# Batch 0: three V chunks normalised on ScalarE, and the magnitudes of six pieces of w_out taken there

## The chip, the cores and the metric

One core of a Trainium2 chip runs the whole program. Its engines are TensorE (PE for matmuls, PEld for weight loads), VectorE (DVE), ScalarE (ACT), GpSimd (POOL) and SyncE (SP, which here issues nearly all DMAs). Each has a queue of its own and runs it strictly in the order in which it was built; the engines meet at semaphores. The metric is the device time of one execution in microseconds.

## What is computed

Three layers run one after the other on 4 batches of 576 rows: windowed causal attention with ALiBi bias (8 heads of 64), a gated MLP with a spatial mix (the part that this change touches), and a second MLP with a three-tap convolution as its gate.

```python
h = gelu(x @ w_in)                       # 512 -> 1024
u, v = h[..., :512], h[..., 512:]
v_n = (v - mean(v)) / np.sqrt(var(v) + 1e-6) * g_ln
v_s = np.einsum('ts,bsd->btd', w_sg, v_n) + b_sg[None, :, None]
x = x + (u * v_s) @ w_out
```

The weights of the matmuls come as float64. The kernel reads their bits as pairs of 32-bit words and makes two fp32r parts of each, high and low, so that a product is three matmuls (high by high, high by low, low by high).

## The kernel before

The rows of `V` of a batch (its 576 positions) are cut into five chunks, `V0.0` to `V0.4` for batch 0: four of 128 rows and a last one of 64 rows. `m_v` makes a chunk: matmuls into a PSUM bank, the gelu on ACT into the tile `v`, mean and variance on DVE (L767, L768), one over the root on POOL (L770, L771, a power of -0.5), `(v - mean) * rs` on DVE in one instruction (L772), and the split: the high part `vn` is a cast on ACT (L223), the low part a subtraction on DVE (L232). The last chunk is first put together from two halves of a bank, by a copy on ACT (L223) and an addition on DVE.

`m_u` makes `u` in halves of 256 and 320 rows with a gelu on ACT from a bank; `m_sg` is the spatial mix (`pss`, evicted by DVE at L829); `m_wo` the product with `w_out` (`pso`). These, and `m_v`, share a pool of two PSUM banks: a group of matmuls can't begin until the bank it gets has been read by an engine. The scores of the attention (`sc`) take banks from another pool, are masked by DVE (L440, with the row maximum) and put through exp on ACT with a row sum; L487 and L488 invert the sums, and POOL and DVE scale the weights by them (L243, tiles `t`).

While batch 0 is in its gated MLP, the weights `w_sg` (five pieces, `g0` to `g4`) and `w_out` (eight pieces of 256 columns, `o0.0` to `o3.1`) are brought in and split between the other steps, and the scores and exps of batch 1 are made. A piece of `w_out` goes through `narrowed`: its high words without sign (L313 on DVE, or L311 on ACT where `act_abs` is set), a clamp (L317), a mask and shift (L318), two steps that put in the sign and the low bits (L319, L320), all on DVE; then a cast on ACT (high part, `wo`) and a subtraction on POOL (low part). The tile `wa` has two buffers, so the first instruction of a piece waits until the piece two before it is through ACT and POOL.

`_steps` lists the order of steps, for batch 0's MLP `g0 g1 V0.2 g2 o0.0 U0.0.3 g3 o0.1 V0.4 ... o1.0 C o1.1 V0.3 o2.0 o2.1 U0.1.0 ...`; from it, the framework's scheduler sets the order of each engine's instructions by a time line of its own, so an edit to one instruction can move its neighbours. `pick` and `book` keep an account of each engine's work, by which some copies and splits choose an engine. The functions follow with the line numbers of the profile.

Of the kernel before, what the change touches and what calls it, by code (L numbers as in the profile page):

```python
# [11 lines left out]
AF = mybir.ActivationFunctionType  # L12
ALU = mybir.AluOpType
# [122 lines left out]
def attention_gmlp_glu_kernel(  # L136
# [21 lines left out]
    nc = tc.nc  # L158
    PSUM = bass.MemoryType.PSUM

    def f(ap):
        return ap.bitcast(F32)

    def pad(pool, n, name):

        if n:
            pool.tile([P, 8 * n], F32, name=name, bufs=1)
# [16 lines left out]
    def act(*args, **kw):  # L184

        book("act", (225 if "accum_out" in kw else 60) + width(args[0]))
        ins = nc.scalar.activation(*args, **kw)  # L187
        if last_act:
            tc.add_manual_dep(ins.ins, last_act[-1], follow, reason="tables")
        last_act.append(ins.ins.name)  # L190
        return ins
# [4 lines left out]
    def width(ap):  # L196
        n = 1
        for d in ap.shape[1:]:
            n *= d
        return n  # L200

    def book(eng, ns):
        load[eng] = max(load[eng], load["pe"] - SLACK) + ns

    def pick(costs):
        eng = min(costs, key=lambda e: max(load[e], load["pe"] - SLACK) + costs[e])
        book(eng, costs[eng])
        return eng

    def mm(out, lhsT, rhs, start, stop, **kw):  # L210
        per = 2 if lhsT.dtype == F32 else 1
        book_pe = max(width(rhs), 2 * width(lhsT) if per == 1 else width(lhsT)) * per / 2.4
        load["pe"] += book_pe
        return nc.tensor.matmul(out, lhsT, rhs, start=start, stop=stop, **kw)  # L214

    def copy(dst, src, psum=False, engines="act dve pool"):
        n = width(src)
        cost = dict(act=52 + 0.85 * n, dve=67 + 1.04 * n) if psum else dict(
            act=20 + 1.0 * n, dve=150 + 0.52 * n, pool=130 + 0.9 * n
        )  # L220
        eng = pick({e: c for e, c in cost.items() if e in engines.split()})
        if eng == "act":
            return nc.scalar.copy(dst, src)  # L223
        if eng == "dve":
            return nc.vector.tensor_copy(dst, src)
        return nc.gpsimd.tensor_scalar(dst, src, 1.0, 1.0, op0=ALU.mult, op1=ALU.mult)  # L226

    def tt(dst, a, b, op, engines="dve pool"):
        n = width(a)
        cost = dict(dve=67 + 1.045 * n, pool=147 + 2.1 * n)  # L230
        eng = pick({e: c for e, c in cost.items() if e in engines.split()})
        return (nc.vector if eng == "dve" else nc.gpsimd).tensor_tensor(dst, a, b, op=op)  # L232
# [12 lines left out]
    def split(hi, lo, src, kind=None, done=None):  # L245

        ins = copy(hi, src, kind is None, ON[kind + " hi"] if kind else "act dve")
        if done is not None:
            done[:] = [ins.ins.name]
        return tt(lo, src, f(hi), ALU.subtract, ON[kind + " lo"] if kind else "dve")  # L250
# [11 lines left out]
    with tc.using_default_side("right"):  # L262
        pa = ExitStack()
        apool = pa.enter_context(tc.tile_pool(name="apool", bufs=2))
# [13 lines left out]
    for i in range(NP):  # L278
        st = cpool.tile([P, 18], F32, name=f"st{i}")
# [19 lines left out]
    def narrowed(src, n, pool, tag, bufs, spool, stag, sbufs, act_abs=False):  # L299

        if spool is None:
            st = src
        else:
            st = spool.tile([P, STAGE[stag]], U32, tag=stag, name="w64", bufs=sbufs)
            dma = nc.sync.dma_start(st[:, : 2 * n], src)
            later(dma)
        words = st[:, : 2 * n].rearrange("p (n w) -> p n w", w=2)
        low, high = words[:, :, 0], words[:, :, 1]
        a = pool.tile([P, 256 if tag == "wa" else 512], U32, tag=tag, name="wa", bufs=bufs)[:, :n]
        if act_abs:  # L310
            tc.keep_in_program_order(nc.scalar.activation(f(a), f(high), AF.Abs))  # L311
        else:
            ins = tc.keep_in_program_order(nc.vector.tensor_scalar(a, high, 0x7FFFFFFF, None, op0=ALU.bitwise_and))  # L313
            if last_hi:
                tc.add_manual_dep(ins.ins, last_hi[-1], follow, reason="high part first")
        clamp = nc.gpsimd if pick({e: c for e, c in dict(dve=67 + 0.52 * n, pool=147 + 0.93 * n).items() if e in ON["clamp"]}) == "pool" else nc.vector
        tc.keep_in_program_order(clamp.tensor_scalar(f(a), f(a), W_LOW, W_HIGH, op0=ALU.max, op1=ALU.min))  # L317
        nc.vector.tensor_scalar(a, a, 0x07FFFFFF, 3, op0=ALU.bitwise_and, op1=ALU.logical_shift_left)  # L318
        nc.vector.scalar_tensor_tensor(a, high, 0xC0000000, a, op0=ALU.bitwise_and, op1=ALU.bitwise_or)  # L319
        nc.vector.scalar_tensor_tensor(a, low, 29, a, op0=ALU.logical_shift_right, op1=ALU.bitwise_or)  # L320
        book("dve", 200 + 2.6 * n)
        return f(a)

    def cols(w, k, c0, n):

        return w.bitcast(U32)[:, k, 2 * c0 : 2 * (c0 + n)]
# [3 lines left out]
    def later(dma):  # L330

        tc.add_manual_dep(dma.ins, last_in[0].ins.name, follow, reason="later")
# [14 lines left out]
    def staged(src, dtype):  # L347
        st = mpool.tile([P, S], dtype, tag="x", name="wst", bufs=8)[:, : src.shape[-1]]
        later(nc.sync.dma_start(st, src))
        return st  # L350
# [11 lines left out]
    def w_out_piece(k, half):  # L362
        if k == half == 0:
            kept["wo"] = w1pool.tile([P, NK, 2, 2, 256], F32R, tag="wo", name="wo")
        st = staged(cols(w_out, k, half * 256, 256), U32)
        a = narrowed(st, 256, apool, "wa", 2, None, "x", 8)
        split(kept["wo"][:, k, half, 0, :], kept["wo"][:, k, half, 1, :], a, "wo")

    p2pool = []
# [365 lines left out]
    def m_v(b, j):  # L735
        ps = gps.tile([P, 512], F32, tag="g", name="psv")

        r = P if j < 4 else 64
        half, o = j // 2 if j < 4 else 1, j % 2 * P
        if j < 4:  # L740
            work = [(a[:, o : o + P], w, P) for k in range(NK) for hi, lo in [xg[b, k, half]] for a, w in ((hi, winh), (hi, winl), (lo, winh))]
            work = [(a, w[:, i // 3, HF:], n) for i, (a, w, n) in enumerate(work)]
        else:
            xt = [mpool.tile([P, 320], F32R, tag="t1", name="xt", bufs=NT1)[:, :P] for _ in range(NK)]
            for k in range(NK):
                copy(xt[k].rearrange("p (a n) -> p a n", a=2), xtail[b, k], engines="pool")
            work = [(xt[k], winh[:, k, HF:], P) for k in range(NK)]
            work += [(xt[k][:, :D], winl[:, k, HF:], D) for k in range(NK)]
        for n, (a, w, rows) in enumerate(work):
            mm(ps[:rows], a, w, start=n == 0, stop=n == len(work) - 1, skip_group_check=j == 4)  # L750
        if j < 4:
            vn = mpool.tile([P, 2, HF], F32R, tag="vn", name="vn", bufs=NVN)
            hi, lo = vn[:, 0, :], vn[:, 1, :]
        else:
            if b == 0:
                pad(mpool, 6, "pad1")
            hi = lo = mpool.tile([P, HF], F32R, tag="vt", name="vn", bufs=1)
        v = mpool.tile([P, HF], F32, tag="v", name="v", bufs=NV)
        if j < 4:
            act(v, ps, AF.Gelu_apprx_tanh)  # L760
        else:
            copy(v[:r], ps[r:], True, "act")
            tt(v[:r], ps[:r], v[:r], ALU.add, "dve")
            act(v[:r], v[:r], AF.Gelu_apprx_tanh)
        bs, ba, rs = small(6, "bs"), small(2, "ba"), small(1, "rs")
        book("dve", 1200)
        nc.vector.bn_stats(bs[:r], v[:r])  # L767
        nc.vector.bn_aggr(ba[:r], bs[:r])  # L768
        book("pool", 800)
        nc.gpsimd.tensor_scalar(rs[:r], ba[:r, 1:2], 1.0, 1e-6, op0=ALU.mult, op1=ALU.add)  # L770
        nc.gpsimd.tensor_tensor(rs[:r], rs[:r], mhalf[:r], op=ALU.pow)  # L771
        nc.vector.tensor_scalar(v[:r], v[:r], ba[:r, 0:1], rs[:r], op0=ALU.subtract, op1=ALU.mult)  # L772
        split(hi[:r], lo if j < 4 else hi[64:], v[:r], "vn first")
        vns[b, j] = (hi, lo)

# [79 lines left out]
    def constants(i):  # L855
# [10 lines left out]
    STEP = dict(  # L866
        k=constants, l=z_load, v=z_vload, c=z_scores, e=z_exp, n=z_norm, t=z_transpose, z=z_av, j=w_in_load, L=a_load, M=a_vload, C=a_scores, E=a_exp, N=a_norm, T=a_transpose, A=a_av,
        X=a_xsplit, V=m_v, U=m_u, G=m_sg, W=m_wo, i=w_in_piece, g=w_sg_piece, o=w_out_piece, a=w2_piece,
    )

# [228 lines left out]
```

## Time and profile before

| | us |
|---|---|
| runs shown (3): lowest, median, highest | 550.97, 551.67, 553.74 |
| the execution that was profiled | 552.74 |
| its span, first to last instruction | 550.7 |

The profiled execution took 552.74 us, 2.04 us more than its span, and 1.07 us more than the median of the three. On the page, busy time is given by engine and share of the span. A timeline gives instructions in order of time, equal neighbours merged, with the idle time of the engine before them and what ended it. A matmul's duration is modelled, and starts of neighbours on one engine may lie closer together than a duration, as writing back overlaps with the next instruction.

### The profile page before, as it was taken

How to read it: one execution, taken by the hardware profiler on the slowest of the kernel's cores; microseconds unless marked ns; L12 is line 12 of the kernel's file. 1: busy time of each engine (PE TensorE's matmuls, PEld its weight loads, DVE VectorE, ACT ScalarE, POOL GpSimd, SP SyncE). 2: the span in 40 equal slices, each digit the busy share in tenths (PEclk: the TensorE clock that was granted, in tenths of full speed). 3: DMA queues.
4: the chain of work that ended last, by engine and by line, in shares of the span. 5: the costliest groups of instructions: out<-in, count | busy, mean ns of one | idle time of the engine just before them, and what ended most of it. 6: DMA issues, size and time to landing. Idle time of an engine off the chain costs nothing.

```text
span 550.7 us, 12017 instructions
## 1 busy us (share of the span) xinstructions
PE 524.9 (95%) x4560; PEld 476.3 (86%) x4560; DVE 371.9 (68%) x955; ACT 263.2 (48%) x681; POOL 249.4 (45%) x379
## 2 busy tenths in 40 slices
PE   8997979999999999999999989998999999999997
PEld 7776778898898988998897979997997999999887
DVE  4999898655869766879766688597577434664300
ACT  6694577342457542376444524473544333444311
POOL 2444239451237262345534344177496454455500
PEclk9999999899999999999999999998999999999999
DMA  8973440333250864322553423901201300100111
GB/s 296 384 245 155 148 153 24 137 119 109 80 182 24 247 201 150 122 80 75 188 186 97 139 87 124 336 8 43 82 18 43 103 21 19 42 20 19 39 38 58
DMA packets 33209, 63.93 MB, mean 116 GB/s; under 512 B 3968, under 2 KB 13952, under 8 KB 33152
## 3 DMA queue, kind: packets, MB, share of 16 engines
q1 hardware_dynamic: 33008, 63.04, 34.4%
q8 instruction: 36, 0.59, 0.4%
q14 instruction: 21, 0.17, 0.1%
q10 hardware_dynamic: 144, 0.13, 0.1%
HBM read 48.47 MB, written 14.68 MB: 115 GB/s over the span
## 4 chain that ended last, share of the span: by engine, by line
PE 47%; DVE 21%; ACT 11%; POOL 10%; DMA 5%; issue 4%; SPq 0%; POOLq 0%; ACTq 0%; DVEq 0%
PE psg L214 26%; PE pso L214 6%; ACT t L187 5%; PE psu L214 4%; DMA x2d<-x 3%; PE psv L214 3%; POOL t L243 3%; PE o L214 3%; POOL gl L232 2%; DVE cc L957 2%; PE sc L214 2%; DVE t L440 2%; PE pss L214 2%; DVE gg L232 2%; PE pT L504 2%
## 5 line engine op out<-in xcount | busy, mean ns | idle before, releaser
L214 PEld LDWEIGHTS psg<-x2g,w 128*128 128x128 f32 x768 | 104.4, 189 | 1.8 <-POOL x2g L226 0.5
L214 PE MATMUL psg<-x2g,w 128*128 128x256 f32 (+1 forms) x768 | 105.8, 295 | 0.1
L214 PE MATMUL psg<-wout,gh 128*128 128x512 f32 (+1 forms) x272 | 80.5, 380 | 1.9 <-ACT gh L223 1.9
L187 ACT ACTIVATE t<-t,st 128x192 f32<-128x192 f32 (+1 forms) x144 | 61.9, 431 | 16.1 <-DVE st L440 16.0
L214 PE MATMUL pss<-wsg,vn 128*128 128x256 f32 (+1 forms) x448 | 63.4, 297 | 3.4 <-DVE t L829 3.0
L214 PEld LDWEIGHTS pss<-wsg,vn 128*128 128x128 f32 x448 | 59.8, 188 | 4.9 <-DVE t L829 4.5
L957 DVE SCALAR_TENSOR_TENSOR cc<-hb,cw,cc 128x576 f32<-128x576 f32 x32 | 28.8, 904 | 46.8 <-POOL cc L243 37.5
L214 PEld LDWEIGHTS psg<-wout,gh 128*128 128x128 f32 x272 | 49.9, 189 | 10.8 <-ACT gh L223 2.1
L214 PE MATMUL psu<-xg,win 128*128 128x320 f32 (+1 forms) x384 | 54.8, 298 | 3.5 <-ACT win L223 1.7
L214 PEld LDWEIGHTS psu<-xg,win 128*128 128x128 f32 x384 | 51.5, 188 | 5.4 <-ACT win L223 1.8
L214 PE MATMUL pso<-gh,wo 128*128 128x256 f32 (+1 forms) x256 | 54.1, 305 | 1.8 <-DVE t L829 1.7
L214 PE MATMUL psg<-wout,gl 128*128 128x512 f32 (+1 forms) x136 | 50.9, 378 | 0.0
L232 POOL TENSOR_TENSOR gl<-gg,gh 128x512 fp32r<-128x512 f32 x32 | 44.7, 1397 | 9.7 <-ACT gh L223 7.5
L214 PE MATMUL psv<-win,xg 128*128 128x512 f32 x192 | 47.7, 398 | 1.0 <-DVE wa L317 0.9
L232 DVE TENSOR_TENSOR gg<-cc,hb 128x576 f32<-128x576 f32 x32 | 33.5, 1048 | 16.7 <-ACT cc L187 16.6
L214 PEld LDWEIGHTS pso<-gh,wo 128*128 128x128 f32 x256 | 41.3, 192 | 3.6 <-DVE t L829 3.1
L243 POOL TENSOR_SCALAR cc<-hb,cw 128x576 f32<-128x576 f32 x26 | 23.5, 904 | 45.5 <-ACT hb L953 44.2
L440 DVE CUSTOM_DVE_ANT_0 t<-sc,tab 128x192 f32<-128x192 f32 (+1 forms) x144 | 40.4, 334 | 5.0 <-PE sc L214 5.0
L214 PEld LDWEIGHTS psv<-win,xg 128*128 128x128 f32 x192 | 35.4, 188 | 8.9 <-ACT win L223 1.0
L953 ACT ACTIVATE hb<-psg 128x576 f32<-128x576 f32 x32 | 20.7, 651 | 44.6 <-PE psg L214 44.6
L214 PE MATMUL pso<-gl,wo 128*128 128x256 f32 (+1 forms) x128 | 38.4, 304 | 2.7 <-DVE gl L232 2.0
L232 POOL TENSOR_TENSOR t<-t,u 128x256 f32<-128x256 f32 (+1 forms) x32 | 26.9, 847 | 22.5 <-DVE t L829 21.9
(103 smaller groups left out, 967.7 us busy)
## 6 DMA issues: line engine op xcount, KB each, us to landing
V<-in_v_dram SPq DMA_DIRECT2D x12, 704.0 KB, 5.0
x2s<-x2d SPq DMA_DIRECT2D x16, 288.0 KB, 3.4
w<-in_w_in_dram SPq DMA_DIRECT2D x8, 512.0 KB, 7.3
w<-in_w_out_dram SPq DMA_DIRECT2D x16, 256.0 KB, 2.9
w<-in_w_in_dram SPq DMA_DIRECT2D x16, 256.0 KB, 2.6
wout<-w2d SPq DMA_DIRECT2D x8, 512.0 KB, 5.6
q<-in_q_dram SPq DMA_DIRECT2D x12, 320.0 KB, 3.9
out_dram<-ot SPq DMA_DIRECT2D x15, 256.0 KB, 2.0
```

The source lines that it names most:

```text
L187: ins = nc.scalar.activation(*args, **kw)
L214: return nc.tensor.matmul(out, lhsT, rhs, start=start, stop=stop, **kw)
L232: return (nc.vector if eng == "dve" else nc.gpsimd).tensor_tensor(dst, a, b, op=op)
L243: e.tensor_scalar(dst, src, col, 1.0, op0=ALU.mult, op1=ALU.mult)
L440: nc.vector.tensor_tensor_reduce(e, bank, table, scale=-SCALE, scalar=3e38, op0=ALU.add, op1=ALU.min, accum_out=mx)
L504: grouped(nc.tensor.transpose(ps[:, i * P : (i + 1) * P], src, ident), first and i == 0, waits if i == 0 else ())
L953: nc.scalar.activation(h[:, 1 : S + 1], ps[:, 256 : 256 + S], AF.Relu)
L957: nc.vector.scalar_tensor_tensor(cc, h[:, 0:S], cw[:, 0, c : c + 1], cc, op0=ALU.mult, op1=ALU.add)
```

## The change

The last three chunks that the order makes in batch 0 (`j > 1`: `V0.2`, `V0.4`, `V0.3`) are normalised on ACT as `Identity(rs * v + nm)`; POOL gets one more instruction for each, `nm = mean * rs * -1`, written over the variance. The pieces of `w_out` with `k < 3`, two halves each and so six pieces, take their magnitude on ACT (`Abs`, L311) in place of L313 on DVE. The new branch puts five lines into `m_v`, so that later lines count five more (L829 is L834, L772's other branch L777).

```diff
@@ w_out_piece
-        a = narrowed(st, 256, apool, "wa", 2, None, "x", 8)
+        a = narrowed(st, 256, apool, "wa", 2, None, "x", 8, k < 3)
@@ m_v
-        nc.vector.tensor_scalar(v[:r], v[:r], ba[:r, 0:1], rs[:r], op0=ALU.subtract, op1=ALU.mult)
+        if b == 0 and j > 1:
+            nm = ba[:, 1:2]
+            nc.gpsimd.tensor_scalar(nm[:r], ba[:r, 0:1], rs[:r], -1.0, op0=ALU.mult, op1=ALU.mult)
+            act(v[:r], v[:r], AF.Identity, bias=nm[:r], scale=rs[:r])
+        else:
+            nc.vector.tensor_scalar(v[:r], v[:r], ba[:r, 0:1], rs[:r], op0=ALU.subtract, op1=ALU.mult)
```

The scheduler moved more than these instructions. The first place is ACT around the gelu of chunk `V0.3`, the first instruction to read that chunk's bank. Before (`v_887`, `v_962` and `v_1057` are the tiles of `V0.2`, `V0.4` and `V0.3`; `psv_1043` is the bank; `wa_906`, `wa_935` are the first two pieces of `w_out`, `wst_982` the last piece of `w_sg`):

```order
L223 CAST vn_886<-v_887 128x512
L187 ACTIVATE v_962<-v_962 64x512
L223 CAST wsg0_863<-wst_982 128x576
L223 CAST wo_903<-wa_906 128x256
L187 ACTIVATE v_1057<-psv_1043 128x512
L187 ACTIVATE u_768<-psu_1095 128x320
```

And now (numbers are one or two higher: `v_963` is `V0.4`, `v_1059` `V0.3`, `wa_907` and `wa_936` the first two pieces, `wa_990` the third):

```order
L223 CAST vn_886<-v_887 128x512
L187 ACTIVATE v_963<-v_963 64x512
L223 CAST wo_904<-wa_907 128x256
L223 CAST wo_904<-wa_936 128x256
L187 ACTIVATE v_963<-v_963,ba_968,rs_969 64x512
L223 CAST wsg0_863<-wst_984 128x576
L311 ACTIVATE wa_990<-wst_988 128x256
L187 ACTIVATE v_1059<-psv_1045 128x512
```

Between the gelu of `V0.4` and that of `V0.3` stood two casts; now five instructions stand there, among them the cast of a second piece and the normalising of `V0.4`.

The second place is DVE, at the addition that puts `V0.4` together (`v<-psv,v`). Before:

```order
L767 BN_STATS bs<-v 128x6
L232 TENSOR_TENSOR wsg_864<-wst,wsg_863 128x576
L313 TENSOR_SCALAR wa<-wst 128x256
L768 BN_AGGR ba<-bs 128x2
L317 TENSOR_SCALAR wa<-wa 128x256
L318 TENSOR_SCALAR wa<-wa 128x256
L232 TENSOR_TENSOR wsg_864<-wst,wsg_863 128x576
L313 TENSOR_SCALAR wa<-wst 128x256
L319 SCALAR_TENSOR_TENSOR wa<-wst,wa 128x256
L772 TENSOR_SCALAR v<-v,ba,rs 128x512
L232 TENSOR_TENSOR v<-psv,v 64x512
```

And now:

```order
L232 TENSOR_TENSOR wsg_864<-wst,wsg_863 128x576 x2
L767 BN_STATS bs<-v 128x6
L768 BN_AGGR ba<-bs 128x2
L232 TENSOR_TENSOR v<-psv,v 64x512
L440 ISA t_86,st_88<-sc,tab 128x128
```

The two low parts of `w_sg` and the first steps of two pieces of `w_out` stood ahead of the addition; they now stand behind it, among the nine masks of the scores (L440).

The third place is DVE from the first eviction of the spatial mix on. Before (`t<-pss,gln,bsg` is the eviction, `r<-st_88` and `r<-st_89` the sums of the exps of head pairs 0 and 1):

```order
L829 SCALAR_TENSOR_TENSOR t_1287<-pss,gln,bsg 128x256
L313 TENSOR_SCALAR wa<-wst 128x256
L317 TENSOR_SCALAR wa<-wa 128x256
L318 TENSOR_SCALAR wa<-wa 128x256
L319 SCALAR_TENSOR_TENSOR wa<-wst,wa 128x256
L829 SCALAR_TENSOR_TENSOR t_1309<-pss,gln,bsg 128x256
L320 SCALAR_TENSOR_TENSOR wa<-wst,wa 128x256
L313 TENSOR_SCALAR wa<-wst 128x256
L317 TENSOR_SCALAR wa<-wa 128x256
L829 SCALAR_TENSOR_TENSOR t_1331<-pss,gln,bsg 128x256
```

And now, from the two rows before it (which stood there before as well):

```order
L487 TENSOR_SCALAR r<-st_88 128x9
L488 RECIPROCAL r<-r 128x9
L834 SCALAR_TENSOR_TENSOR t_1290<-pss,gln,bsg 128x256
L834 SCALAR_TENSOR_TENSOR t_1312<-pss,gln,bsg 128x256
L834 SCALAR_TENSOR_TENSOR t_1334<-pss,gln,bsg 128x256
```

All eight pieces of `w_out` are now ahead of the masks of head pair 2 and so of the first eviction, where five were before; the last three stood between evictions. On PE two matmuls change places with neighbours; after the MLP of batch 0 the order of every engine is what it was.

## Rows read from the trace of the kernel before

**Rows 1.** The page's head: span, busy time of each engine.
```profile
span 550.7 us, 12017 instructions
...
PE 524.9 (95%) x4560; PEld 476.3 (86%) x4560; DVE 371.9 (68%) x955; ACT 263.2 (48%) x681; POOL 249.4 (45%) x379
```

**Rows 2.** Windows of 10 us: start:end, length, busy PE, PEld, DVE, ACT, POOL, clock, DMA.
```profile
70.00:80.00 10.00, 7.91 (x87) 7.24 (x86) 9.01 (x36) 7.86 (x25) 3.19 (x6) 1.00 0.37 121
80.00:90.00 10.00, 8.33 (x66) 7.91 (x65) 9.79 (x41) 9.71 (x43) 8.59 (x16) 1.00 0.25 88
90.00:100.00 10.00, 8.80 (x99) 7.67 (x98) 8.15 (x19) 3.94 (x11) 10.00 (x19) 0.98 0.23 75
```

**Rows 3.** Timeline of PE: start, us, engine, line, operation, count, [idle before <-releaser].
```profile
57.97 2.01 PE L214 MATMUL psv<-win,xt 128*128 128x512 f32 x8
...
64.50 3.68 PE L214 MATMUL psu<-xg,win 128*128 128x320 f32 x24
...
76.89 1.41 PE L214 MATMUL sc<-k,q 64*64 64x192 f32 x24 [2.09 <-DVE st L440]
...
83.15 6.02 PE L214 MATMUL pss<-wsg,vn 128*128 128x256 f32 x42 [1.54 <-DVE t L829]
...
99.46 0.45 PE L214 MATMUL pso<-gl,wo 128*128 128x256 f32 x1 [0.33 <-POOL gl L232]
```

**Rows 4.** Timeline of DVE, same columns.
```profile
57.85 0.69 DVE L767 BATCH_NORM_STATS2 bs<-v 128x6 f32<-128x512 f32 x1
...
62.00 0.54 DVE L772 TENSOR_SCALAR v<-v,ba,rs 128x512 f32<-128x512 f32 x1
...
62.45 0.68 DVE L232 TENSOR_TENSOR v<-psv,v 64x512 f32<-64x512 f32 x1
...
69.82 0.28 DVE L318 TENSOR_SCALAR wa<-wa 128x256 uint32<-128x256 uint32 x1
...
71.88 0.96 DVE L772 TENSOR_SCALAR v<-v,ba,rs 128x512 f32<-128x512 f32 x1 [0.46 <-POOL rs L771]
...
77.21 0.29 DVE L317 TENSOR_SCALAR wa<-wa 128x256 f32<-128x256 f32 x1
...
79.97 0.28 DVE L440 CUSTOM_DVE_ANT_0 t<-sc,tab 128x128 f32<-128x128 f32 x1
...
82.67 0.42 DVE L829 SCALAR_TENSOR_TENSOR t<-pss,gln,bsg 128x256 f32<-128x256 f32 x1
```

**Rows 5.** Timeline of ACT, same columns.
```profile
60.08 0.67 ACT L223 CAST wsg<-wst 128x576 fp32r<-128x576 f32 x1 [1.47 <-DMA wst<-in_w_sg_dram]
...
60.78 0.58 ACT L223 COPY v<-psv 64x512 f32<-64x512 f32 x1
...
65.11 0.60 ACT L187 ACTIVATE v<-psv 128x512 f32<-128x512 f32 x1
...
74.78 1.28 ACT L187 ACT_TABLE_LOAD   x1
...
80.53 0.40 ACT L187 ACTIVATE t<-t,st 128x128 f32<-128x128 f32 x1
```

**Rows 6.** Timeline of POOL, same columns.
```profile
69.43 1.09 POOL L771 TENSOR_TENSOR rs<-rs,mhalf 64x1 f32<-64x1 f32 x1
...
82.86 4.20 POOL L243 TENSOR_SCALAR t<-t,r 128x128 f32<-128x128 f32 x9 [1.41 <-DVE r L488]
...
89.57 2.71 POOL L243 TENSOR_SCALAR t<-t,r 128x128 f32<-128x128 f32 x7
...
92.94 1.43 POOL L232 TENSOR_TENSOR wo<-wa,wo 128x256 fp32r<-128x256 f32 x2
```

**Rows 7.** Line 311 over the whole span: min/median/max ns, first and last start, forms.
```profile
L311 ACT ACTIVATE wa<-w x17: 422/437/687, 13.1 to 337.2; 128x256 f32<-128x256 f32 x12, 128x512 f32<-128x512 f32 x5
```

**Rows 8.** Windows of 2 us, columns as in rows 2.
```profile
100.00:102.00 2.00, 2.00 (x11) 2.00 (x11) 1.23 (x3) 0.46 (x1) 2.00 (x3) 0.50 0.00 0
102.00:104.00 2.00, 2.00 (x41) 1.73 (x41) 0.42 (x1) 0.37 (x1) 0.32 (x1) 0.74 0.29 99
```

## The prediction

> **What bounds the kernel now.** The page's head comes first: TensorE is busy 95% of the span, VectorE 68%, ScalarE 48%, GpSimd 45% [rows 1]. A change can only gain what TensorE loses to waits, and it costs time wherever it makes TensorE wait. The change lies in one stretch, so the windows come next. Between 70 and 100 us TensorE is busy 7.91, 8.33 and 8.80 of each 10 us, VectorE 9.01, 9.79 and 8.15, ScalarE 9.71 in the second window, GpSimd all of the third [rows 2]. The reader is to see that here TensorE is not the limit: VectorE is until the first eviction of the spatial mix at 82.67 [rows 4], then GpSimd. The timeline of TensorE names the waits: 2.09 us for a mask before 76.89, 1.54 us for the eviction before 83.15, and short ones on GpSimd, the last before 99.46 [rows 3]. From there on it runs almost without a gap for a long time, so a delay of the batch's `pso` products should be carried to the end.
>
> **What the change takes away.** VectorE loses three normalisations, 0.54 to 0.96 us each, the longer one with a 0.46 us wait for GpSimd ahead of it [rows 4], and six magnitudes of about 0.28 us, priced by the L318 row of that size [rows 4]. That is 0.54 + 0.54 + 0.96 + 1.7 = 3.7 us, and about 0.9 us of waits, counting the second short chunk's wait like the one shown. ScalarE gains six magnitudes of 0.43 us, the median of the line [rows 7], and three normalisations. No row shows an Identity with two column operands; the nearest are the copy of 0.58 and the gelu of 0.60 [rows 5], so between 0.58 and, with half again for the operands, 0.9; I take 0.6, the value of the rows. GpSimd gains three operations on one column: the nearest row is the power at 1.09 us [rows 6], so between 0.1 and 1.1; I take 0.3, as the new one has no power in it. By duration the trade looks fair. The order decides otherwise.
>
> **Step 1: VectorE stands at the addition.** The copy that starts chunk V0.4 now comes on ScalarE directly behind the gelu of V0.2, and needs the matmuls that end at 57.97 + 2.01 = 59.98 [rows 3]. It ends at about 60.0 + 0.58 = 60.6 (before, it began at 60.78 [rows 5]). VectorE, done with the statistics of V0.2 at 57.85 + 0.69 and the short aggregate at about 58.7 [rows 4], has nothing ahead of the addition any more and stands some 1.9 us; its two low parts of `w_sg` and two pieces of `w_out` are queued behind it.
>
> **Step 2: ScalarE stands behind VectorE.** From the addition to its L318 at 69.82 VectorE worked 7.37 us without a break before [rows 4]. The new list from the addition to the last step of the first piece is nearly the same work (nine masks, one low part of `vn`, the statistics); against it, one more low part of `w_sg` and one small operation come in, one statistics and about three small ones go, so 7.0 to 7.3. The piece is ready at 60.6 + 7.2 = 67.8. ScalarE stood idle for it since its gelu of V0.4. The cast of the first piece begins at 67.8, that of the second after two more VectorE steps, at about 68.6.
>
> **Step 3: then behind GpSimd.** The normalising of V0.4 is next on ScalarE. GpSimd, from the aggregate at about 67.5, does the variance column (0.3), the power (1.09 [rows 6]), the low part of the first piece, which now stands ahead of the new column, at half of 1.43 [rows 6], and the new column (0.3): 67.5 + 0.3 + 1.09 + 0.72 + 0.3 = 69.9. ScalarE then does the normalising (0.6), the cast of `w_sg` (0.67 [rows 5]), the third magnitude (0.43 [rows 7]) and only then the gelu of V0.3 (0.60): done at 72.2, with overlaps about 72.0. Before, it began at 65.11 [rows 5].
>
> **Step 4: TensorE stands for a bank.** Behind V0.3 come the first two groups of `u` of the second half, 24 matmuls in 3.68 us from 64.50 [rows 3]. The second group gets V0.3's bank, so it waits for that gelu: from 64.50 + 1.84 = 66.3 to 72.0, 5.7 us. Behind it in TensorE's queue are the scores of head pair 1, two more groups of `u` and the scores of pair 2. Of these 5.7 us at most 2.09 + 1.54 = 3.6 can be taken out of later waits [rows 3].
>
> **Step 5: the first eviction comes late.** VectorE's list from about 71.1 (the last low part of `w_sg`) to the masks of pair 2 now holds all the remaining pieces. Between 69.82 and 79.97 [rows 4] it did nine masks, two low parts of `vn` and 13 steps of pieces: 10.15 less the waits (0.9), the two normalisations (1.5) and 0.4 of a slowed low part is 7.3. The new list has 26 steps of pieces, 13 more at 2.76 / 10 = 0.28 (77.21 to 79.97 holds nine steps and a mask [rows 4]), 3.6, and a low part, statistics and an aggregate, 1.5: 12.4, to 83.5. The pieces now go round ScalarE, VectorE, ScalarE, GpSimd with two buffers, so I add 1 us of waits: 84.5. The nine masks and the inverse take 2.7, as from 79.97 to 82.67 [rows 4], so by VectorE alone the eviction comes at 87.2, not 82.67: 4.5 late. ScalarE is later still. Its last gelu of `u` stands behind the cast of the seventh piece, one chain of five steps ahead of 84.5, so 83.1 + 0.4 + 0.4 = 84 (before, the table load began at 74.78 [rows 5]). The load takes 1.28, the exps of pair 0 80.53 - 76.06 = 4.5 less one cast that has moved, 4.1 [rows 5]: 89.4. The inverse of their sums, two short instructions, stands on VectorE ahead of the eviction, where it cost nothing while the exps were early. So the eviction comes at 89.8 to 90, 7.3 late; the bounds are 4.5 and 8.3.
>
> **Step 6: what is given back.** Behind the eviction GpSimd is the limit, from 82.86 to the end of that window [rows 2, 6]. It loses two low parts of pieces there, 1.43 us. With VectorE's pieces gone, its nine scalings of pair 0 could fall from 4.20 / 9 = 0.47 to the 2.71 / 7 = 0.39 of pair 1 [rows 6], 0.7 more. Here the Trainium skill can be weighed (SBUF — State Buffer, "Who interferes with whom"): a VectorE operation in a two-port mode and a GpSimd operation exclude each other for a whole instruction, which would give the 0.7 in full. The rows show unequal times without saying that this is why, so I take the 1.43 alone: 7.3 - 1.4 = 5.9 late at the `pso` products.
>
> TensorE's granted clock was 0.50, the lower level of 1.2 GHz, in 100 to 102 us and 0.74 in the next two [rows 8], after the broken run of short `pso` waits. At 2.4 GHz that stretch would be 2 x 0.50 + 2 x 0.26 = 1.5 us shorter. After the change the stretch may keep the higher level (-1.5), or lose as much again behind the long waits (+1.5). I take half of the gain: 5.9 - 0.7 = 5.2 us.
>
> **Sum.** The profiled execution took 552.74, so 557.9; it is 1.07 above the median of the runs shown, 551.67, and against that the forecast is 556.9, put at 557.0. Later parts keep their order and I give them nothing.
>
> **Rivals.**
> Faster: VectorE was the limit from 70 to 83 us, 3.7 us of work goes, and the two waits of 3.6 us and the slow-clock stretch of 1.5 vanish: 551.7 - 3.6 = 548.1, at best 546.6. For it speaks that VectorE is at 9 of 10 and ScalarE was at half before 70. Against it: ScalarE must reach the gelu of V0.3 by 66.3, and its order puts five instructions before it that need VectorE's late steps. The Trainium skill (Perfetto Trace Analysis, "Optimizing Scalar/DVE Operations") has the rule that would bring this about: where VectorE is saturated, giving work to ScalarE may pay. By that rule, 548; rows 2 show the saturation, and the order the reason why I doubt it. Chance 0.08.
> No change: the gelu is late, but by no more than the 3.6 us of later waits, and GpSimd's chain then starts on time. That needs the sums of pair 0 by 83, so a table load by 77. 551.7, give or take 2.7. Chance 0.12.
> Slower by less or more (forecast): 557.0, by step 5's place and price; it decides once the exps of pair 0 end after 82.3. Its own range is 552.6 (4.5 - 1.4 - 0.7 - 1.5 = +0.9) to 560.1 (8.3 - 1.4 + 1.5 = +8.4). Chance 0.80.
> That the change doesn't do what it says would be a second pair of table loads, for Identity or Abs outside the gelu's set: 2 x 1.28 = 2.6 us on ScalarE [rows 5], 559.6. The built order has no load there, so it is 0.02 within the forecast's share.
>
> **How the numbers follow.** Half a per cent, 2.8 us, is about what a measurement of this kernel can tell from no change: faster is under 548.9, slower over 554.4. From the cases: 0.08, 0.13 (with a sliver of the forecast's low end) and 0.79. The range of 553.0 to 560.5 leaves out the faster case and most of no change.
>
> **What would show it.** In the new profile: the copy of V0.4 at 60.0 and VectorE idle before 60.6; ScalarE idle from 64 to 68 for a piece's L320; the gelu of V0.3 ending near 72 and TensorE waiting over 5 us for it before `psu`; the table load near 84; the first eviction near 90; GpSimd's first scaling right before it, seven or eight us late. It is wrong if that gelu starts before 67, if the exps of pair 0 end before 84, or if the delay at `pso` isn't found again at the end.

## The result and the profile after

The changed kernel took 559.96 us (median; 558.68 to 561.24) against 552.38 us of the kernel before (550.86 to 554.46): a ratio of 1.0143, 95% interval 1.0116 to 1.017, so 7.6 us slower by the medians. The forecast was 557.0 in a range of 553.0 to 560.5. One execution of experiment `e5` below, the one profiled, and one of the kernel before beside it took 1294 us; the ratio leaves them out, the medians don't (`e5` has 557.23 us without its own), and `e8` gives the trace in its place.

The page's head of the changed kernel stands against [rows 1]: VectorE is 0.9 us less busy and ScalarE 3.7 us more, TensorE 1.4 us more, and none of it is near the 8.2 us by which the span grew.

```profile
span 558.9 us, 12027 instructions
...
PE 526.3 (94%) x4560; PEld 478.0 (86%) x4560; DVE 371.0 (66%) x946; ACT 266.9 (48%) x690; POOL 248.7 (44%) x382
```

Before two timelines are laid beside each other, their origins have to agree. ScalarE's second table load comes long before the change and has the same neighbours in both. First the kernel before, then the one after (start, us, engine, line, operation):

```profile
37.76 1.28 ACT L187 ACT_TABLE_LOAD   x1
```

```profile
38.94 1.28 ACT L187 ACT_TABLE_LOAD   x1
```

So 1.2 us is taken off every time after (and between -0.1 and 1.2 off those of the experiments, by the same row); "shifted" below means this. With that, one window of 50 us of each kernel shows the damage, first before, then after (columns as in [rows 2]):

```profile
60.00:110.00 50.00, 45.04 (x511) 41.44 (x512) 42.00 (x149) 29.82 (x97) 26.82 (x45) 0.97 0.36 117
```

```profile
61.17:111.17 50.00, 38.51 (x380) 35.98 (x381) 36.89 (x123) 31.47 (x98) 24.38 (x46) 0.86 0.29 92
```

TensorE worked 6.5 us less in the same 50 us, and VectorE, which was to be relieved, 5.1 us less too: both stood. ScalarE alone did more. Three rows of TensorE's timeline after say for whom it stood; they answer to the `psu` row and the waits of [rows 3].

```profile
65.67 1.92 PE L214 MATMUL psu<-xg,win 128*128 128x320 f32 x12
73.34 3.57 PE L214 MATMUL psu<-xg,win 128*128 128x320 f32 x12 [5.75 <-ACT v L187]
...
94.44 7.38 PE L214 MATMUL pss<-wsg,vn 128*128 128x256 f32 x41 [4.62 <-DVE t L834]
```

The 24 `psu` matmuls that ran together before are cut in two: twelve run, then TensorE waits 5.75 us for ScalarE to free V0.3's bank. The second wait, 4.62 us, is for the first eviction of the spatial mix, which had cost 1.54. The reader should also see the durations: the second twelve `psu` take 3.57 us where the first took 1.92. The windows name the reason, with the clock as the last but two of the columns:

```profile
72.00:74.00 2.00, 0.66 (x2) 0.66 (x3) 1.49 (x4) 1.80 (x4) 0.00 (x0) 0.50 0.06 23
74.00:76.00 2.00, 2.00 (x9) 2.00 (x9) 1.87 (x6) 0.00 (x1) 0.64 (x2) 0.50 0.38 131
76.00:78.00 2.00, 2.00 (x28) 1.67 (x30) 1.16 (x3) 1.95 (x5) 1.34 (x3) 0.50 0.34 120
...
96.00:98.00 2.00, 2.00 (x11) 2.00 (x11) 0.16 (x1) 2.00 (x11) 2.00 (x6) 0.50 0.00 0
...
100.00:102.00 2.00, 2.00 (x17) 1.99 (x16) 1.86 (x8) 1.39 (x7) 1.76 (x5) 1.00 0.00 0
```

After each of these two stands the granted clock is 0.50, the level of 1.2 GHz, and stays there while TensorE is already fully busy again. The dip of before at 100 to 104 [rows 8] is gone.

ScalarE's timeline after shows what held the gelu of V0.3 (it answers to [rows 5]):

```profile
65.10 0.63 ACT L187 ACTIVATE v<-v 64x512 f32<-64x512 f32 x1
68.96 0.41 ACT L223 CAST wo<-wa 128x256 fp32r<-128x256 f32 x1 [3.22 <-DVE wa L320]
...
71.10 0.81 ACT L187 ACTIVATE v<-v,ba,rs 64x512 f32<-64x512 f32 x1 [0.94 <-POOL ba L774]
71.82 0.65 ACT L223 CAST wsg<-wst 128x576 fp32r<-128x576 f32 x1
72.38 0.42 ACT L311 ACTIVATE wa<-wst 128x256 f32<-128x256 f32 x1
72.71 0.57 ACT L187 ACTIVATE v<-psv 128x512 f32<-128x512 f32 x1
...
87.11 0.41 ACT L223 CAST wo<-wa 128x256 fp32r<-128x256 f32 x1 [1.65 <-DVE wa L320]
87.42 0.43 ACT L187 ACTIVATE u<-psu 128x320 f32<-128x320 f32 x1
87.87 1.28 ACT L187 ACT_TABLE_LOAD   x1
```

The gelu of V0.3 starts at 72.71, or 71.5 shifted, instead of 65.11. Ahead of it stand the casts of two pieces, the normalising of V0.4 and what they wait for. The matmuls into its bank had ended by 65.67, where the first `psu` starts.

### The profile page after: what moved, and what is told of

Read it like the earlier page. It is cut to its first block, busy times and chain, and to the rows that moved or that the text cites. A ratio compares the mean times of both kernels' runs of the same rounds, so it can differ in the third digit from the quotient of the medians.

```text
span 558.9 us, 12027 instructions
## 1 busy us (share of the span) xinstructions
PE 526.3 (94%) x4560; PEld 478.0 (86%) x4560; DVE 371.0 (66%) x946; ACT 266.9 (48%) x690; POOL 248.7 (44%) x382
## 4 chain that ended last, share of the span: by engine, by line
PE 53%; DVE 20%; ACT 11%; POOL 7%; issue 4%; DMA 4%; SPq 0%; POOLq 0%; ACTq 0%; DVEq 0%
PE psg L214 25%; PE pso L214 7%; ACT t L187 4%; PE psu L214 4%; PE pss L214 4%; PE o L214 4%; PE sc L214 3%; PE psv L214 3%; PE pT L504 2%; DVE cc L962 2%; DMA x2d<-x 2%; POOL gl L232 2%; DVE gg L232 2%; DVE t L440 1%; DVE cc L963 1%
## 5 line engine op out<-in xcount | busy, mean ns | idle before, releaser
L214 PE MATMUL pss<-wsg,vn 128*128 128x256 f32 (+1 forms) x448 | 65.4, 303 | 7.1 <-DVE t L834 5.7
L214 PEld LDWEIGHTS pss<-wsg,vn 128*128 128x128 f32 x448 | 61.8, 194 | 8.9 <-DVE t L834 6.9
L214 PE MATMUL psu<-xg,win 128*128 128x320 f32 (+1 forms) x384 | 56.7, 304 | 9.4 <-ACT v L187 6.1
L214 PEld LDWEIGHTS psu<-xg,win 128*128 128x128 f32 x384 | 53.0, 193 | 11.7 <-ACT v L187 6.5
L214 PE MATMUL pso<-gh,wo 128*128 128x256 f32 (+1 forms) x256 | 52.8, 301 | 1.1 <-DVE t L834 1.0
L440 DVE CUSTOM_DVE_ANT_0 t<-sc,tab 128x192 f32<-128x192 f32 (+1 forms) x144 | 40.3, 335 | 6.2 <-PE sc L214 6.2
```

The lines of the kernel that those rows point to most:

```text
L440: nc.vector.tensor_tensor_reduce(e, bank, table, scale=-SCALE, scalar=3e38, op0=ALU.add, op1=ALU.min, accum_out=mx)
```

## The order behind it

The prediction read this place off the built order and asked no further. The code has the reason: the gelus, the exps and the sigmoid are issued through `act()` (the copies and the Abs aren't), and `act()` ties each one to the one before it (`add_manual_dep(ins.ins, last_act[-1], follow, reason="tables")`), so that ScalarE runs these functions in the order of the program. The change issues the new Identity through `act()` too. From then on the scheduler may not place the gelu of V0.3 ahead of the normalising of V0.4, though nothing in the data asks for that, and this normalising hangs on VectorE's statistics and GpSimd's power. This is theory A. Its rival B: the moved work itself (the Identity, GpSimd's third step, the Abs) is what costs.

## The experiments

Times of before in the same runs: 551.41 us for the first four, 552.52 for e5 to e7, 552.05 for e8 and e9. Ratios are against those, with 95% intervals; they are formed from the executions and are not the quotients of the medians. `e1`, `e4` and `e9` have four executions each, `e8` one, the others ten.

**The normalisings alone** (`e1`: the changed kernel, magnitudes left on VectorE).

```diff
-        a = narrowed(st, 256, apool, "wa", 2, None, "x", 8, k < 3)
+        a = narrowed(st, 256, apool, "wa", 2, None, "x", 8)
```

> Only the normalising of the three chunks goes to ScalarE, the magnitudes of w_out stay on VectorE. Theory A (order): Identity is issued through the helper that chains all of ScalarE's activations in program order, so the gelu of V0.3 has to stand behind the normalising of V0.4, which waits for VectorE and GpSimd. The chain is still there, with one cast of a piece and no magnitude ahead of the gelu: TensorE still waits for that gelu, about 2 to 4 us, and the time is 2 to 5 us over the kernel before. Rival B (work): the pieces of w_out that now go round ScalarE, VectorE, ScalarE, GpSimd with two buffers are what delays; then this kernel is within 2 us of before.

557.13 us, ratio 1.0116 (1.0063 to 1.017). TensorE's timeline has the same wait, and ScalarE's the same place for the normalising of V0.4:

```profile
72.73 3.57 PE L214 MATMUL psu<-xg,win 128*128 128x320 f32 x12 [5.71 <-ACT v L187]
...
88.95 5.62 PE L214 MATMUL pss<-wsg,vn 128*128 128x256 f32 x42 [1.67 <-DVE t L834]
```

```profile
70.51 0.81 ACT L187 ACTIVATE v<-v,ba,rs 64x512 f32<-64x512 f32 x1 [6.01 <-POOL ba L774]
...
72.09 0.59 ACT L187 ACTIVATE v<-psv 128x512 f32<-128x512 f32 x1
```

So the first wait belongs to the normalisings; I had put it too low. The second wait is that of before: in the changed kernel its other 3 us come with the magnitudes.

**The magnitudes alone** (`e2`: an edit of the kernel before).

```diff
-        a = narrowed(st, 256, apool, "wa", 2, None, "x", 8)
+        a = narrowed(st, 256, apool, "wa", 2, None, "x", 8, k < 3)
```

> Only the six magnitudes go to ScalarE; the normalising stays on VectorE. Theory A: nothing but gelus and exps is in the chain, so the gelu of V0.3 starts near 65 us as before, and the time is within 2 us of before. Rival B: the pieces' longer round delays the table load and the first eviction by 5 us or more, and the time is 4 us or more over before.

552.26 us, ratio 1.0019 (0.9998 to 1.004): no difference. Its gelu of V0.3 starts at 65.14 and its table load at 74.75, as in [rows 5], and TensorE waits 1.63 us for the first eviction. So the magnitudes bring the other 3 us of that wait only together with the normalisings in the chain.

**The normalisings outside the chain** (`e3`: the changed kernel, same instructions, another way of issuing).

```diff
-            act(v[:r], v[:r], AF.Identity, bias=nm[:r], scale=rs[:r])
+            book("act", 60 + width(v))
+            nc.scalar.activation(v[:r], v[:r], AF.Identity, bias=nm[:r], scale=rs[:r])
```

> The whole change, but Identity is issued outside the chain of activations (same books, no dependence on the activation before it), so that the scheduler may put the gelu of V0.3 and those of u ahead of the normalising of V0.4. Same instructions on every engine as in the change. Theory A: the wait of TensorE for the gelu of V0.3 (5.8 us) and the one for the first eviction (4.6 us) go, and the time falls to that of the kernel before or some 2 us under it: 548 to 553. Rival B: the work is the same, so 557 to 561.

552.3 us, ratio 1.0018 (0.9993 to 1.0043). All the work of the change is in this kernel and the 7.6 us are gone. ScalarE's timeline (the Identity's line is now 776):

```profile
67.41 0.60 ACT L187 ACTIVATE v<-psv 128x512 f32<-128x512 f32 x1
...
71.08 0.81 ACT L776 ACTIVATE v<-v,ba,rs 64x512 f32<-64x512 f32 x1
```

The gelu goes ahead of the normalising, and the wait at `psu` is gone. But nothing is won either, and of its two waits theory A had only the first right. TensorE still waits for the eviction, and takes 7.13 us for the 42 matmuls behind it (6.02 before; the granted clock in 86 to 88 is 0.50), and VectorE waits for a magnitude that the scheduler has put among the exps:

```profile
84.88 7.13 PE L214 MATMUL pss<-wsg,vn 128*128 128x256 f32 x42 [4.15 <-DVE t L835]
```

```profile
83.81 0.29 DVE L317 TENSOR_SCALAR wa<-wa 128x256 f32<-128x256 f32 x1 [2.66 <-ACT wa L311]
```

**The first evictions ahead of the inverse** (`e4`: the changed kernel; the inverse of pair 0's sums, which waits for the exps, is put behind the first two evictions on VectorE).

```diff
+        GN = [f"E{of(p)}"] + G[0][:2] + [f"N{of(p)}"] + G[0][2:]
-        gw = weigh(p) + G[0] + weigh(p + 1) + G[1][:1] + loads(p + 3) + T[:1] + G[1][1:2] + W[0][:1] + A[:1] + halves(p)
+        gw = (GN if b == 0 else weigh(p) + G[0]) + weigh(p + 1) + G[1][:1] + loads(p + 3) + T[:1] + G[1][1:2] + W[0][:1] + A[:1] + halves(p)
...
-        nc.vector.tensor_scalar_add(r, s["sm"], 1e-9)
+        ins = nc.vector.tensor_scalar_add(r, s["sm"], 1e-9)
+        if (b, m) == (1, 0):
+            tc.add_manual_dep(ins.ins, mixed[1].ins.name, follow, reason="evictions first")
```

> The whole change with ScalarE's order as it is, but the inverse of the sums of head pair 0 is put behind the first two evictions on VectorE, so that they no longer wait for the exps. If that wait costs what the trace shows it for (4.6 us on TensorE), the first eviction comes at about 91 in place of 94 us and two groups of the spatial mix start sooner; GpSimd's scaling can start no sooner, so I expect 1 to 3 us less than the change: 557 to 559. Rival: the end is set by the exps and GpSimd alone, and nothing is gained: 560.

561.36 us, ratio 1.0181 (1.0142 to 1.0219): no gain, as its rival had it. On shifted times the first eviction does come at 90.2 instead of 92.8, but TensorE stands at the next place:

```profile
90.97 5.61 PE L215 MATMUL pss<-wsg,vn 128*128 128x256 f32 x42 [2.06 <-DVE t L838]
99.33 3.41 PE L215 MATMUL pss<-wsg,vn 128*128 128x320 f32 x14 [2.75 <-DVE t L838]
```

One wait of 4.62 has become two of 4.8 together, and the scores of pair 3 start at 115.9 shifted, against 115.5 in the changed kernel. The inverse ahead of the eviction, of which step 5 made a point, decides where TensorE waits and not for how long.

**The wait alone** (`e5`, and `e8` for its trace: the kernel before, VectorE normalises, nothing is moved; the next function in the chain waits for each of the last three normalisings of batch 0).

```diff
     def act(*args, **kw):
         ...
         last_act.append(ins.ins.name)
+        while normed:
+            tc.add_manual_dep(ins.ins, normed.pop(), behind, reason="normalised first")
...
-        nc.vector.tensor_scalar(v[:r], v[:r], ba[:r, 0:1], rs[:r], op0=ALU.subtract, op1=ALU.mult)
+        ins = nc.vector.tensor_scalar(v[:r], v[:r], ba[:r, 0:1], rs[:r], op0=ALU.subtract, op1=ALU.mult)
+        if b == 0 and j > 1:
+            normed.append(ins.ins.name)
```

> The kernel before with the added wait alone: VectorE normalises all chunks as before, no ScalarE operation is added, but ScalarE's activation that follows each of the last three V chunks of batch 0 in the chain (the gelu of V0.3, and the gelus of u) has to wait for that chunk's normalising on VectorE. Theory A (the time goes by the place of the normalising in ScalarE's chain of activations, not by the work that is moved): TensorE's first psu of the next u tile waits 5 to 7 us for ScalarE's gelu of V0.3, as in the changed kernel, the table load comes 5 to 9 us later than at 74.8, and the time is 555.5 to 559. Rival B (the moved work itself, the 0.81 us Identity and GpSimd's third step, costs it): none of that work is here, so 551 to 553.

> The same kernel as the added wait alone, for its trace. Theory A: the psu wait for ScalarE's gelu of V0.3 is 4 to 7 us and the table load comes at 80 to 84 (its time is 4.0 us above before, against 7.6 of the change, so about half of the changed kernel's lateness). Rival B: no such wait, the 4 us lie elsewhere.

557.57 us, ratio 1.0073 (1.0043 to 1.0103), so 2.4 to 5.7 us slower by the wait alone; the single run of `e8` took 556.82. TensorE's and ScalarE's rows of `e8` (lines shifted by two):

```profile
72.46 3.57 PE L216 MATMUL psu<-xg,win 128*128 128x320 f32 x12 [5.54 <-ACT v L187]
```

```profile
71.29 0.62 ACT L225 CAST vn<-v 64x512 fp32r<-64x512 f32 x1 [6.00 <-DVE v L774]
71.82 0.58 ACT L187 ACTIVATE v<-psv 128x512 f32<-128x512 f32 x1
...
82.62 1.28 ACT L187 ACT_TABLE_LOAD   x1
```

The gelu stands behind VectorE's normalising of V0.4 (L774 here). TensorE's wait is 0.2 us short of the changed kernel's, with none of its work. B falls as the whole cause. The table load is at 82.1 shifted, between the 74.8 of before and the changed kernel's 86.7; the part that is missing has the magnitudes and the Identities in it.

**The normalisings outside the chain without magnitudes** (`e6`), **and with five in place of six** (`e7`): each an edit of `e3`.

```diff
-        a = narrowed(st, 256, apool, "wa", 2, None, "x", 8, k < 3)
+        a = narrowed(st, 256, apool, "wa", 2, None, "x", 8)
```

```diff
-        a = narrowed(st, 256, apool, "wa", 2, None, "x", 8, k < 3)
+        a = narrowed(st, 256, apool, "wa", 2, None, "x", 8, k + half < 3)
```

> The three normalisings on ScalarE as in the change, but outside the chain of activations, and no magnitude of w_out on ScalarE. Theory A: the gelu of V0.3 goes ahead of the normalising of V0.4 (start 65 to 68 instead of 72), no psu wait over 1 us, time 550.5 to 553 against 551.4 before. Rival B: the work costs what it cost with the chain, 555.5 to 558.

> Normalising outside the chain and the magnitudes of five pieces of w_out instead of six on ScalarE (the sixth, which stood among the exps of pair 0 and kept VectorE waiting 2.66 us, stays on VectorE). Theory A: that wait goes, the first eviction comes 1.5 to 2.5 us earlier than the 84.35 of the kernel with six, time 550 to 552, so at most 1 us better than before. Rival C (another wait takes its place, the exps and GpSimd's scaling set the eviction): 552 to 553, no change against six.

`e6` took 552.32 us, ratio 0.9999 (0.9972 to 1.0025), its gelu of V0.3 at 65.10; `e7` 552.35, ratio 0.9985 (0.9956 to 1.0014). In `e7` the wait of 2.66 us is gone and the eviction comes at 83.63, 82.5 shifted, against 83.9 shifted in `e3`: 1.4 earlier, a little under the 1.5 to 2.5 expected. But TensorE arrives earlier by as much and waits as long as in `e3`, and VectorE, right ahead of the eviction, now waits for the exps:

```profile
84.16 7.67 PE L214 MATMUL pss<-wsg,vn 128*128 128x256 f32 x42 [4.19 <-DVE t L835]
```

```profile
83.55 0.17 DVE L487 TENSOR_SCALAR r<-st 128x9 f32<-128x9 f32 x1 [0.23 <-ACT t L187]
```

The time is the same, as rival C of `e7` had it: the exps set the eviction. In all three free versions work has left VectorE and no time has been won.

**V0.4 left on VectorE** (`e9`: an edit of the changed kernel).

```diff
-        if b == 0 and j > 1:
+        if b == 0 and j in (2, 3):
```

> The change with V0.4 (the 64-row chunk) left on VectorE; V0.2 and V0.3 are normalised by ScalarE inside the chain, the six magnitudes stay. Theory A (what costs is that the gelu of V0.3 stands behind the normalising of V0.4): the gelu of V0.3 starts at 65 to 68, no psu wait over 1.5 us; the normalising of V0.3 still holds back the gelus of u, by 1 to 2 us, in a wait that is short; time 552 to 555. Rival C (any normalising in the chain costs as much, so V0.3's does the same to the gelus of u): 557 to 560.

557.55 us, ratio 1.0116 (1.008 to 1.0153). I was wrong here; rival C's range holds. The gelu of V0.3 does start early, at 67.67, and its wait shrinks to 1.46. But the next member of the chain takes over: V0.3's normalising waits for GpSimd, with the gelus of `u` behind it, and TensorE for those. TensorE first, then ScalarE:

```profile
68.31 2.02 PE L214 MATMUL psu<-xg,win 128*128 128x320 f32 x12 [1.46 <-ACT v L187]
75.09 5.32 PE L214 MATMUL psu<-xg,win 128*128 128x320 f32 x24 [2.86 <-ACT u L187]
```

```profile
73.90 0.81 ACT L187 ACTIVATE v<-v,ba,rs 128x512 f32<-128x512 f32 x1 [1.52 <-POOL ba L774]
74.62 0.74 ACT L187 ACTIVATE u<-psu 128x320 f32<-128x320 f32 x2
```

So it isn't only that V0.4 stands in the wrong place. V0.3's normalising, which waits for VectorE and GpSimd too, holds back the chain at its own place, and TensorE's banks hang on the gelus behind either.

## Why the prediction was right, and where it was off

**Steps 1 and 2** held. VectorE stood 1.87 us at the addition (forecast 1.9). ScalarE got its first piece at 68.96, 67.8 shifted, as forecast.

**Step 3** held to 0.1 us: the gelu of V0.3 was due to end at about 72.0 and ended at 73.28, 72.1 shifted. Two of its terms were off in ways that cancelled: GpSimd's power took 0.73 where 1.09 was taken, and the column ahead of it 0.61 where 0.3 was. A third, the Identity, took 0.81 where I took 0.6, inside the bounds of 0.58 to 0.9. On that operation the Trainium skill (ScalarE: Activation LUTs, "What ACT_TABLE_LOAD costs") would have done better: each column operand adds about 93 ns, an estimate of 0.60 + 0.19 = 0.79, with which the trace's 0.81 agrees.

**Step 4** held: 5.75 us for the bank against 5.7. It left out that TensorE had a granted clock of 0.50, 1.2 GHz, after this stand: the twelve `psu` took 3.57 instead of 1.92, 1.65 more.

**Step 5** is the term that was mis-sized. The first eviction was forecast 7.3 us late, with a bound of 8.3. It came at 93.96, 92.8 shifted, against 82.67: 10.1 late, outside that bound. The window of VectorE's list after and its rows show the missing 2.8:

```profile
72.51:88.99 16.48, 14.53 (x151) 13.37 (x152) 15.10 (x49) 7.97 (x18) 5.01 (x8) 0.83 0.38 125
```

```profile
72.51 0.76 DVE L232 TENSOR_TENSOR wsg<-wst,wsg 128x576 fp32r<-128x576 f32 x1 [2.79 <-ACT wsg L223]
...
76.77 0.83 DVE L317 TENSOR_SCALAR wa<-wa 128x256 f32<-128x256 f32 x1 [0.81 <-ACT wa L311]
...
80.34 0.29 DVE L317 TENSOR_SCALAR wa<-wa 128x256 f32<-128x256 f32 x1
80.66 0.29 DVE L318 TENSOR_SCALAR wa<-wa 128x256 uint32<-128x256 uint32 x1
80.99 0.43 DVE L319 SCALAR_TENSOR_TENSOR wa<-wst,wa 128x256 uint32<-128x256 uint32 x1
81.45 0.42 DVE L320 SCALAR_TENSOR_TENSOR wa<-wst,wa 128x256 uint32<-128x256 uint32 x1
81.79 0.35 DVE L440 CUSTOM_DVE_ANT_0 t<-sc,tab 128x192 f32<-128x192 f32 x1
...
85.25 0.83 DVE L318 TENSOR_SCALAR wa<-wa 128x256 uint32<-128x256 uint32 x1
...
87.64 0.97 DVE L319 SCALAR_TENSOR_TENSOR wa<-wst,wa 128x256 uint32<-128x256 uint32 x1
...
93.45 0.35 DVE L487 TENSOR_SCALAR r<-st 128x9 f32<-128x9 f32 x1 [2.01 <-ACT t L187]
93.96 0.82 DVE L834 SCALAR_TENSOR_TENSOR t<-pss,gln,bsg 128x256 f32<-128x256 f32 x2
```

The list began at 72.51, 71.3 shifted, where 71.1 was forecast. It was priced at 0.28 us a step, from nine steps that lay among others. A piece whose steps follow each other, each on the result of the last, takes 81.79 - 80.34 = 1.45 for four, 0.36 a step. Three steps took 0.83 to 0.97 instead of 0.29 to 0.43, 0.54 more each and 1.6 together. GpSimd's rows at the same times show what ran beside them:

```profile
76.71 0.74 POOL L232 TENSOR_TENSOR wo<-wa,wo 128x256 fp32r<-128x256 f32 x1
...
85.20 0.73 POOL L232 TENSOR_TENSOR wo<-wa,wo 128x256 fp32r<-128x256 f32 x1 [2.06 <-ACT wo L223]
87.59 0.74 POOL L232 TENSOR_TENSOR wo<-wa,wo 128x256 fp32r<-128x256 f32 x1 [1.66 <-ACT wo L223]
```

Each of the three long steps began 0.05 or 0.06 us after GpSimd had begun the low part of a piece, and ended after it. Two more low parts in this stretch (79.46 and 82.39) met masks and a step of 0.38. No run isolates this, so it is a coincidence in time and not a shown cause; but it, and not the dependence of the steps, goes with more than half of the 2.7 us by which the list was busier than forecast. In all, the list was busy for 15.1 us, not 12.4, with 1.4 of stands where I had 1.0: 3.1 more. The seventh piece's cast, ahead of the last gelu of `u` and the table load, came at 87.11, 85.9 shifted, and not at 83.1: the same 2.8. The rest of step 5 then followed as written: the load at 86.7 shifted, the exps behind it, and VectorE standing 2.01 us for them at the inverse, at 93.45, right ahead of the eviction.

**Step 6**: from the first eviction to the scores of pair 3 took 107.59 - 82.67 = 24.9 us before and 116.66 - 93.96 = 22.7 after, so 2.2 came back, with 2.1 forecast (1.43 and 0.7 of the clock). That the two agree is in part luck. GpSimd, by contrast to [rows 6], has no low part of `w_out` left there, as forecast, and its nine scalings took 0.39 each:

```profile
94.15 3.54 POOL L243 TENSOR_SCALAR t<-t,r 128x128 f32<-128x128 f32 x9 [0.38 <-DVE r L488]
```

That is the 0.66 us which the prediction weighed under the rule of the Trainium skill (SBUF — State Buffer, "Who interferes with whom") and left out. It came while VectorE worked for 0.63 of these 3.54 us; before, at 0.47 a scaling, VectorE worked for 4.06 of the 4.20 us, and in `e9`, at 0.42, for 2.12 of 3.77. These agree with the rule, but no run changes VectorE's work alone, so they aren't proof. The clock, whose 0.7 was counted, gave nothing net: its old dip is gone, but 41 `pss` took 7.38 us against 6.02 for 42. Nor is GpSimd the limit there any more, though step 6 had it so: from 94.44 to the scores of pair 3 at 116.66 TensorE shows no wait, and the chain that ended last runs on TensorE alone. So pair 3 was 10.1 - 2.2 = 7.9 us late, where 5.2 was forecast; the difference is step 5's. It was carried on: the last table load of the span came at 363.42, 362.2 shifted, against 353.81, 8.4 late; at the end 7.6 of it is found in the medians.

The rivals: "faster" failed at the place named against it, ScalarE's order, and the experiments add that even without the chain the work moved off VectorE buys nothing (e3, e6, e7). "No change" failed as the table load came at 86.7 shifted, far from the 77 it needed. The cause that the prediction lacked is the chain; it saw its effect in the order and so had the right sign and the wrong depth of reason.

What stays open is how the difference between the wait alone (ratio 1.0073) and the change (1.0143), some 4 us, divides among the pieces' way round the engines, the moved work behind the wait and the slow clock. The magnitudes add some 2 us to the normalisings by the medians and 3 us to TensorE's wait for the eviction, but the intervals of `e1` and of the change overlap, and `e9` has the magnitudes and two normalisings in the chain without that longer wait (1.67 us).

## What to carry to other kernels

Before an operation goes to an idle engine, look at what will stand behind it in that engine's queue, and whether the way it is issued ties it to neighbours that its data does not. An operation that waits for two other engines must not stand ahead of one that frees a TensorE bank. And price a chain of dependent small steps by rows of such a chain, not by the mean of steps that lay among others, with a look at what another engine does in the same moments.

## What was not expected of the hardware

ScalarE's Identity with a scale and a bias column took 0.81 us both for 64x512 and for 128x512, the gelu of the same chunks, without them, 0.57 to 0.63. After TensorE had stood for 5.75 us, its granted clock was 0.50 in the windows from 72 to 78, and it was busy for all of the last two of them. The same wait with the same 3.57 us for twelve `psu` returns in `e1` and `e8`.
